# Two chunks' attention outputs times their weights by Strassen's product instead of a plain one, in a kernel of two attention branches

## The chip, the cores and the metric

The kernel runs on one NeuronCore of one Trainium2 chip. The metric is the device time of one execution in microseconds (us), lower is better. The engines are TensorE (PE in the profile; PEld is its weight loading), VectorE (DVE), ScalarE (ACT), GpSimd (POOL) and SyncE (SP), whose queue issues the DMAs.

## The reference

There are two branches over 2048 tokens of width 1024 and 32 heads of 32; their outputs are put side by side. Branch A is the Infini-attention of four segments, not touched here but for its last product `o @ wo`. Branch B is linear attention with a learned feature map:

```python
qkv = (x @ wqkv).reshape(B, S, 3, H, Dh).transpose(2, 0, 3, 1, 4)
q, k, v = qkv[0], qkv[1], qkv[2]
pq = einsum("bhsd,hdf->bhsf", q, w_phi);  pk = einsum("bhsd,hdf->bhsf", k, w_phi)
phi_q = concatenate([softmax(pq), softmax(-pq)], -1)
phi_k = concatenate([softmax(pk), softmax(-pk)], -1)
kv = einsum("bhsf,bhsd->bhfd", phi_k, v);  z = einsum("bhsf->bhf", phi_k)
num = einsum("bhqf,bhfd->bhqd", phi_q, kv)
den = einsum("bhqf,bhf->bhq", phi_q, z)[..., None] + 1e-6
b = (num / den).transpose(0, 2, 1, 3).reshape(B, S, D) @ wo        # the product that changes
return concatenate([a, b], -1)
```

Everything is float32. The kernel splits each float32 operand into two float16 halves, a rounded high one and the rest, and multiplies high by high, high by low and low by high: three products for one.

## The kernel before

**Order.** The work is not written in program order. Every instruction is handed to a planner (`Graph`) with an engine, an assumed duration, a priority `prio` (lower goes first) and the buffers that it reads and writes. `G.run()` simulates the engines with these durations and writes out each engine's instructions in the order that it finds. On the chip every engine then runs its list strictly in that order. The planner also gives out the eight PSUM banks: each request has a kind (`proj`, `misc`, `s`, `pv`, `kv`), `MOST` limits how many of a kind may be held (3, 2, 3, 1, 4) and `KEEP` holds one back for each of the first four. Buffers with the same tag are used in turn; the last number of `G.buf` says how many there are.

**Stages.** First comes branch A's attention, whose output is left in DRAM (`oa_d`). Then come branch B's keys and values (the K stage): 8 pairs `p` of 128-token chunks, each with two Strassen products (keys, then values, for p = 0 to 5; keys alone for 6 and 7), the two-sided softmax of the keys (`expo`), and the sums over tokens of features times values (L1264). Then its queries (the Q stage): 16 chunks `c`. Last is branch A's output product in 8 pairs of chunks, by Strassen's product (L1499).

**Strassen's product here** (Winograd's form): two chunks of 128 rows give a left matrix of 2 x 2 blocks of 128 x 512 (A11, A12, A21, A22), the weights give 2 x 2 blocks of 512 x 512. Seven products of 12 matmuls take the place of eight. They need the forms A11, A12, A22, S1 = A21 + A22, S2 = S1 - A11, S3 = A11 - A21, S4 = A12 - S2, and, of the weights, B11, B21, B22, T1 to T4. Results are gathered in three banks X, Y, Z; intermediate sums are copied out (`keep`) and joined with a later bank (`store`). The query, key and value products (`strassen`, matmuls on L549) and branch A's output have this form already.

**The Q stage.** For an even c the query product of chunks c and c + 1 is made in three `proj` banks. Its priority is P - 1.2 with P = Q0 + c. For each of the four blocks (chunk, half of the heads `hb`) `expo` makes the exponentials `e` (5 buffers) on VectorE and ScalarE. Then per chunk and half: GpSimd multiplies `e` with the key sums (L1414), VectorE reduces (L1417), GpSimd finishes the denominators and scales `e` (L1426), ScalarE and VectorE split it into halves `eh` (tag `kls`, L1432 and L1434), two DMA transposes bring it into `pt` (3 buffers, L1437), and TensorE multiplies it with the key-value sums into a bank `pn` of kind `pv` (L1445). ScalarE and VectorE take `pn` as halves into `ot` (4 buffers, one per chunk, L1449 and L1451). When both halves of the heads are there, `project` multiplies the chunk's 128 x 1024 output with both column halves of `wo` (`product`, matmuls on L359): 2 x 8 x 3 = 48 matmuls of 512 columns. ScalarE copies each bank to `os` (L1329), and SyncE stores it. The priority of `project` is P + 1.1.

**Weights.** `keep_bo(n)` runs in the K stage at p = 1 and 2, once for each column half of branch B's `wo`. It loads 2 MB in two loads to find the scale (absolute sums on ScalarE, L1201), loads them again, makes 8 pairs of halves (`halves`: ScalarE on L386, VectorE on L388, into `kls`) and stores them to `bo_d` (L1210). Before the Q stage they are loaded into slots S4 to S7. Branch A's forms are made in the Q stage (`sizes_out` at c = 1 to 4, `weights` at c = 5, 7, 9, 11; `forms` on L458, L465 and L466): B11, B21 and T1 directly in slots S10, S13 and S14, the other four through `wo_d` in DRAM, loaded at c = 14 (L1402).

## Time and profile before

| | us |
|---|---|
| median of 3 runs | 1761.08 |
| lowest and highest run | 1757.87, 1761.38 |
| the profiled execution, its own time | 1762.63 |
| the profiled execution, its span in the trace | 1760.8 |
| busy in that span: TensorE, VectorE | 1692.6, 1404.1 |
| busy in that span: ScalarE, GpSimd | 1129.7, 968.4 |

In the rows a group of instructions reads: line, engine, operation, written and read tiles, shapes, how many | busy us in total, mean ns of one | idle time of that engine just before them, and what ended it. A row of engines by stage reads: stretch, its length, then the busy us and instructions of each engine, the clock that TensorE was granted (1.00 is full), the share of time that the DMA engines were busy, and GB/s. A row of the timeline reads: start, length, engine, line, operation, how many [idle time before, and its cause]. In a row of waits stand the total us, how many there were and the longest. Matmuls of 512 columns are listed with some 380 ns each, but they overlap: the busy time of a group, divided by its number, is what one costs.

### The profile page before, as it was taken

What the parts mean: (1) busy time and instruction counts of PE and PEld (TensorE: products, weight loads), DVE (VectorE), ACT (ScalarE), POOL (GpSimd) and SP (SyncE); (2) the same over time, 40 slices, a digit from 0 to 9 for tenths busy, and PEclk for the clock granted to TensorE, in tenths of its full rate; (3) what the DMA queues carried; (4) which work ended last, traced back from release to release, by engine and by line L of the source; (5) the groups of instructions that cost most, each with busy time, mean ns of one, the idle gap of its engine ahead of it and who ended that gap; (6) DMA issues with size and microseconds to landing.
All of it is one profiled execution on the core that took longest, in us unless ns stands there. A gap on an engine that the chain in (4) does not pass through costs nothing.

```text
span 1760.8 us, 38488 instructions
## 1 busy us (share of the span) xinstructions
PE 1692.6 (96%) x14456; PEld 1013.5 (58%) x14456; DVE 1404.1 (80%) x3207; ACT 1129.7 (64%) x2063; POOL 968.4 (55%) x1301
## 2 busy tenths in 40 slices
PE   8999999999999999999989999999899999989999
PEld 5767666667776766766744444444444444444444
DVE  5989989899777888788875998996988777677541
ACT  6887886978776787777774656554665544444431
POOL 6445454555757577866773535553578989650000
PEclk8999999999999999999999999999999999999999
DMA  5546546475445444567456343346646666665311
GB/s 191 183 147 178 143 144 182 150 219 170 145 137 152 119 134 122 152 197 184 129 183 254 114 140 137 138 146 236 225 138 168 156 164 147 141 187 159 120 66 66
DMA packets 240842, 275.67 MB, mean 157 GB/s; under 512 B 137488, under 2 KB 190480, under 8 KB 231952
## 3 DMA queue, kind: packets, MB, share of 16 engines
q1 hardware_dynamic: 240656, 273.22, 51.0%
q8 instruction: 113, 1.85, 0.4%
q14 instruction: 73, 0.60, 0.1%
HBM read 145.44 MB, written 85.00 MB: 131 GB/s over the span
## 4 chain that ended last, share of the span: by engine, by line
PE 58%; DVE 19%; ACT 5%; POOL 3%; issue 2%; DMA 1%; SPq 0%; ACTq 0%; DVEq 0%
PE proj L359 19%; PE proj L549 9%; PE proj L1499 5%; PE misc L359 5%; PE s L865 3%; PE pv L901 3%; PE s L767 2%; PE s L1499 2%; DVE s L773 2%; PE s L549 2%; DVE mx L1110 2%; DVE S L388 2%; DVE r L1120 1%; POOL e L1414 1%; PE misc L1499 1%
## 5 line engine op out<-in xcount | busy, mean ns | idle before, releaser
L359 PE MATMUL proj<-S,S 128*128 128x128 f16 (+1 forms) x3072 | 504.0, 300 | 5.2 <-ACT S L386 3.3
L359 PEld LDWEIGHTS <-S 128*128 128x128 f16 x4608 | 331.8, 99 | 154.8 <-issue 10.7
L549 PE MATMUL proj<-S,S 128*128 128x512 f16 x1488 | 351.0, 384 | 17.9 <-ACT cs L555 5.7
L549 PEld LDWEIGHTS <-S 128*128 128x128 f16 x1968 | 189.0, 99 | 237.9 <-issue 19.6
L878 POOL TENSOR_SCALAR_AFFINE_SELECT ph<-ph 128x256 f16<-128x256 f16 (+1 forms) x448 | 196.2, 459 | 178.8 <-DVE ph L872 142.7
L872 DVE SCALAR_TENSOR_TENSOR ph<-s,ph 128x512 f16<-128x512 f32 x320 | 210.5, 682 | 62.1 <-ACT ph L871 60.1
L773 DVE CUSTOM_DVE_ANT_0 s<-s,causal 128x512 f32<-128x512 f32 (+3 forms) x512 | 242.1, 509 | 12.2 <-PE s L767 8.7
L869 ACT ACTIVATE s<-s,bd 128x512 f32<-128x512 f32 x320 | 212.7, 712 | 24.5 <-PE s L865 24.1
L871 ACT ACTIVATE ph<-s 128x512 f16<-128x512 f32 x320 | 190.8, 657 | 1.2 <-PE pv L901 0.5
L359 PE MATMUL misc<-S,ot 128*128 128x512 f16 x768 | 171.7, 381 | 1.5 <-ACT ot L1449 0.9
L1117 ACT ACTIVATE e<-e,sk 128x256 f32<-128x256 f32 x256 | 114.8, 498 | 77.9 <-DVE e L1114 76.7
L359 PEld LDWEIGHTS <-ot 128*128 128x128 f16 x768 | 73.8, 98 | 91.5 <-DVE ot L1451 2.0
L767 PE MATMUL s<-S 96*128 96x512 f16 (+3 forms) x512 | 113.3, 300 | 6.0 <-DVE mt L773 4.2
L865 PE MATMUL s<-S 104*128 104x512 f16 (+3 forms) x512 | 114.4, 302 | 1.9 <-ACT S L795 0.8
L1414 POOL TENSOR_TENSOR e<-e,zb 128x512 f32<-128x512 f32 x64 | 81.6, 1284 | 50.3 <-DVE r L1120 49.7
L359 PE MATMUL proj<-wv,S 128*128 128x128 f16 x1536 | 104.3, 221 | 0.3 <-DVE mt L773 0.3
L901 PEld LDWEIGHTS <-ph 128*128 128x128 f16 x2560 | 87.8, 96 | 19.0 <-POOL ph L878 2.4
L901 PE MATMUL pv<-vl,ph 128*128 128x66 f16 (+1 forms) x2560 | 93.0, 185 | 2.5 <-POOL ph L878 1.6
L1120 DVE TENSOR_REDUCE r<-e 128x32 f32<-128x1024 f32 x64 | 76.8, 1204 | 10.1 <-ACT e L1117 9.8
L549 PE MATMUL s<-S,S 128*128 128x512 f16 x324 | 76.3, 379 | 0.0
L719 ACT ACTIVATE h<-proj,bd 128x512 f16<-128x512 f32 x64 | 47.6, 748 | 44.0 <-PE proj L359 43.8
L773 DVE DVE_READ_ACCUMULATOR2_ANT mt<- 128x1 f32 x512 | 71.9, 140 | 0.0
(313 smaller groups left out, 3268.9 us busy)
## 6 DMA issues: line engine op xcount, KB each, us to landing
S<-h SPq DMA_DIRECT2D x192, 128.0 KB
S<-wf_d SPq DMA_DIRECT2D x21, 1024.0 KB
st<-bwqk SPq DMA_DIRECT2D x64, 256.0 KB
wf_d<-fo SPq DMA_DIRECT2D x48, 256.0 KB
out<-os SPq DMA_DIRECT2D x40, 256.0 KB
wf_d<-oT SPq DMA_DIRECT2D x36, 256.0 KB
S<-xf_d SPq DMA_DIRECT2D x9, 1024.0 KB
S<-aw SPq DMA_DIRECT2D x16, 512.0 KB
```

The source lines that it names most:

```text
L359: op(PE, dur, lambda c=c, a=a, b=b, lv=lv, rv=rv: nc.tensor.matmul(pv(), lv(), rv(), start=(c == 0 and a + b == 0), stop=(c == n - 1 and a ...
L549: op(PE, 0.215, lambda n=n, a=a, b=b, lv=lv, rv=rv: nc.tensor.matmul(ps(), lv(), rv(), start=(start and n == 0 and a + b == 0), stop=(n == ...
L767: nc.tensor.matmul(ps()[:, o:o + 128 * i + 128], st()[0:96, 0, h, 128 * i:128 * i + 128], st()[0:96, 1, h, 0:128 * i + 128], start=True, s ...
L773: dve(0.12 + 0.00113 * n, lambda h=h, i=i, o=o, n=n: nc.vector.tensor_tensor_reduce(ps()[:, o:o + n], ps()[:, o:o + n], causal[:, 512 - n: ...
L865: nc.tensor.matmul(ps()[:, o:o + n], st()[0:104, 1, h, 128 * j:128 * j + 128], st()[0:104, 0, h, 128 * j:512], start=True, stop=True)
L869: act(0.59, lambda: nc.scalar.activation(ps(), ps(), AF.Exp, bias=0.0, scale=bd()[:, 4, i2, 0:1]), r=[(bd, i2)], w=[ps])
L871: act(0.5, lambda: nc.scalar.activation(ph()[:, 0], ps(), AF.Copy, scale=2.0 ** 14), r=[ps], w=[(ph, 0)])
L872: dve(0.6, lambda: nc.vector.scalar_tensor_tensor(ph()[:, 1], ps(), 2.0 ** 14, ph()[:, 0], op0=OP.mult, op1=OP.subtract), r=[ps, (ph, 0)], ...
L878: nc.gpsimd.affine_select(pd, pd, pattern=[[0, n], [1, 128]], compare_op=OP.is_ge, fill=0.0, base=0, channel_multiplier=-1)
L901: nc.tensor.matmul(ps()[:, i, n0:n1], ph()[:, a, o:o + 128], vl()[:, j, h, n0:n1], start=(i == 0 and a == 0), stop=(j == min(i, 2)), skip_ ...
L1117: op(ACT, 0.41, lambda i=i: nc.scalar.activation(e()[:, 4 * i:4 * i + 4], e()[:, 4 * i:4 * i + 4], AF.Exp, bias=0.0, scale=sk()[:, i:i + 1 ...
L1499: op(PE, 0.215, lambda n=n, a=a, b=b: nc.tensor.matmul(ps(), v(a)[:, n, :], wform[w]()[:, b, n, :], start=(start and n == 0 and a + b == 0 ...
```

## The change

- Branch B's output product takes two chunks at a time, in Strassen's form, with the same `project` as branch A's (the body of A's loop moves into it): 7 x 12 = 84 matmuls for two chunks in place of 96, in banks `misc`, `misc` and `s`. Its `keep` copies go to `os` and `kva`. It runs after an odd chunk.
- The forms are made where `pn` lies, now a bank of kind `kv`. Even chunk: each of the two banks is copied to plain float32 (A11 in `kva`, A12 in `ez`) and taken as halves. Odd chunk: the first bank is copied (A21, in a `pt` buffer), turned into S3 by a sum in place and taken; the second is taken as A22 and then turned by three sums in place into S1, S2 and S4, each taken in turn. `take` is the same pair of instructions as before (ScalarE, VectorE); a pair now has seven of them and uses all four `ot` buffers.
- Branch B's weights need seven forms. `sizes_bo` (at p = 0) finds one scale for the whole of `wo`; `weights_bo(j)` (at p = 1 to 4) loads 1 MB, makes seven pairs of halves with four sums on GpSimd, and stores each form's part to `bo_d`. Seven loads of 1 MB into slots KS follow where four were.
- All seven of branch A's weights' forms go through `wo_d`, and all seven are loaded at c = 14, into the slots VS that held the queries' weights.

The core of the diff:

```diff
-    def keep_bo(n, prio):
-        ... (2 x 4 absolute sums; 2 x 4 halves; 2 stores of 1 MB)
+    def sizes_bo(prio):
+        tw = G.buf("b", [128, 16], F32, "ast", 1)
+        for q in range(4):
+            raw = G.buf("b", [128, 4, 512], F32, "zb")
+            ... (load of 1 MB, four absolute sums in place)
+        scale((tw, tw), 16, (wscs, (1, 0), lambda: wsc[:, 1, 0]), prio, "pv", 13)
+    def weights_bo(j, prio):
+        raw = G.buf("b", [128, 4, 512], F32, "zb")
+        for k in range(2):
+            op(SP, 0.6, ... nc.sync.dma_start(raw()[:, 2 * k:2 * k + 2]..., bwo[:, j + 4 * k, :]), ...)
+        def dst(f):
+            ... (kept: one of four places of a "kls" buffer; then a store to bo_d[f, :, :, j, :])
+        forms(WPLAN, lambda k: (raw, k, lambda: raw()[:, k]), dst, (wscs, (1, 0), ...), prio)
...
-        if p in (1, 2):
-            keep_bo(p - 1, P + 0.5)
+        if p == 0:
+            sizes_bo(P + 0.5)
+        if 1 <= p < 5:
+            weights_bo(p - 1, P + 0.5)
...
+    def project(form, wform, kinds, tags, rows, col, sc, prio):
+        ... (mult, keep, store: as in branch A's loop before)
+        X, Y, Z = (bank(k, [128, 512]) for k in kinds)
+        mult(X, "A11", "B11", True)
+        mult(Y, "A12", "B21", True)
+        p1 = keep(X, tags[0])
+        store(p1, rows[0], 0, Y)
+        mult(X, "S2", "T2", False)
+        u2 = keep(X, tags[1])
+        mult(Z, "S1", "T1", True)
+        p5 = keep(Z, tags[2])
+        mult(X, "S3", "T3", False)
+        store(p5, rows[1], 512, X)
+        mult(Z, "S4", "B22", False)
+        store(u2, rows[0], 512, Z)
+        mult(X, "A22", "T4", False)
+        store(keep(X, tags[3]), rows[1], 0)
...
+            for i, f in enumerate(FORMS):
+                wform[f] = G.buf("slot", [128, 2, 4, 512], F16, f"S{VS[i]}")
...
+        def take(ps, f):
+            ... (the next half of an "ot" buffer)
+            op(ACT, 0.48, lambda: nc.scalar.activation(v(0), ps(), AF.Copy, scale=2.0 ** -15), ...)
+            op(DVE, 0.6, lambda: nc.vector.scalar_tensor_tensor(v(1), ps(), 2.0 ** -15, v(0), op0=OP.mult, op1=OP.subtract), ...)
+        def sums(ps, a, b, o):
+            op(DVE, 0.6, lambda: nc.vector.tensor_tensor(ps(), a(), b(), op=o), ...)
+        def plain(ps, tag):
+            t = G.buf("b", [128, 4, 128], F32, *tag)
+            op(ACT, 0.48, lambda: nc.scalar.activation(t(), ps(), AF.Copy), ...)
...
-            pn = bank("pv", [128, 4, 128])
+            pn = bank("kv", [128, 4, 128])
...
+            if c % 2 == 0:
+                if hb == 0:
+                    A11 = plain(pn, ("kva",))
+                    take(pn, "A11")
+                else:
+                    A12 = plain(pn, ("ez",))
+                    take(pn, "A12")
+            elif hb == 0:
+                A21 = plain(pn, ("pt", 3))
+                sums(pn, A11, pn, OP.subtract)
+                take(pn, "S3")
+            else:
+                take(pn, "A22")
+                sums(pn, A21, pn, OP.add)
+                take(pn, "S1")
+                sums(pn, pn, A11, OP.subtract)
+                take(pn, "S2")
+                sums(pn, A12, pn, OP.subtract)
+                take(pn, "S4")
-        project(lambda a, g: (ot, None, ...), bo, c * 128, 1024, P + 1.1)
+        if c % 2:
+            project(form, bof, ("misc", "misc", "s"), (("stage", "os", 1), ("b", "kva", 1), ("stage", "os", 1), ("stage", "os", 1)),
+                    (c - 1, c), 1024, (wo2b, lambda: wo2), P + 1.1)
```

More of the change, by code (lines that the diff above doesn't have):

```diff
@@ new lines, in sizes_bo @@
+        scale((tw, tw), 16, (wscs, (1, 0), lambda: wsc[:, 1, 0]), prio, "pv", 13)
+    def weights_bo(j, prio):
+        raw = G.buf("b", [128, 4, 512], F32, "zb")
+        for k in range(2):
+            op(SP, 0.6, lambda k=k: nc.sync.dma_start(raw()[:, 2 * k:2 * k + 2].rearrange("p a b -> p (a b)"), bwo[:, j + 4 * k, :]),
+               w=[(raw, 2 * k), (raw, 2 * k + 1)], prio=prio, lat=1.0, kb=512)
+        made = []
+        def dst(f):
+            if len(made) % 4 == 0:
+                kept = G.buf("b", [128, 4, 2, 512], F16, "kls")
+            else:
+                kept = made[-1]
+            i = len(made) % 4
+            made.append(kept)
+            return *((kept, (i, a), lambda a=a: kept()[:, i, a]) for a in range(2)), lambda: op(
+                SP, 0.6, lambda: nc.sync.dma_start(bo_d[f, :, :, j, :], kept()[:, i]), r=[(kept, (i, a)) for a in range(2)],
+                w=[(bob, (f, j))], prio=prio, lat=1.5, kb=256)
+        forms(WPLAN, lambda k: (raw, k, lambda: raw()[:, k]), dst, (wscs, (1, 0), lambda: wsc[:, 1, 0]), prio)
@@ L1321, in zv @@
     def zv():
         return zb().rearrange("p a (two s d) -> p (a two) s d", two=2, s=2)
-    def project(o, w, row, col, prio):
-        for n in range(2):
-            ps = bank("misc", [128, 512])
-            product((ps, ps), o, at(w[n]), NG, prio, dur=0.215)
-            os = G.buf("stage", [128, 512], F32, "os", 1)
-            op(ACT, 0.6, lambda os=os, ps=ps, n=n: nc.scalar.activation(os(), ps(), AF.Copy, scale=wo2[:, n:n + 1]),
-               r=[ps, wo2b], w=[os], prio=prio)
-            op(SP, 0.6, lambda os=os, n=n: nc.sync.dma_start(
-                out[row:row + 128, col + 512 * n:col + 512 * n + 512], os()), r=[os], prio=prio, lat=1.5)
@@ L1334, in tile_kernel @@
[L1334 to L1339 removed]
+    FORMS = ("B11", "B21", "T2", "T1", "T3", "B22", "T4")
```

139 lines of the change are left out of this document (60 added, 79 removed).

## The prediction, made before any run of the changed kernel

> **What bounds the kernel now.** I read the page's first part, then the busy time of each engine by stage, then groups of instructions, then the chain of work. The stages, by which lines run when: attention up to about 960 us; the keys' features (K stage) to about 1262, its last pairs overlapped by the first query products; the queries with the projection (Q stage) to 1611; the other branch's output product to the end.
>
> ```profile
> PE 1692.6 (96%) x14456; PEld 1013.5 (58%) x14456; DVE 1404.1 (80%) x3207; ACT 1129.7 (64%) x2063; POOL 968.4 (55%) x1301
> ...
> core 0: us, PE busy (x) PEld busy (x) DVE busy (x) ACT busy (x) POOL busy (x), PEclk, DMA share, GB/s
> 960.00:1180.00 220.00, 205.70 (x1356) 100.77 (x1355) 204.08 (x333) 130.15 (x264) 105.94 (x96) 0.99 0.36 128
> 1222.00:1611.00 389.00, 369.81 (x2494) 178.45 (x2492) 315.60 (x481) 201.97 (x377) 267.86 (x296) 0.99 0.62 170
> ...
> 1050.00:1095.00 45.00, 41.24 (x256) 19.74 (x255) 39.84 (x68) 26.55 (x59) 22.01 (x20) 0.96 0.46 158
> 1095.00:1138.00 43.00, 39.36 (x272) 19.25 (x269) 42.85 (x70) 25.11 (x48) 20.41 (x21) 1.00 0.40 141
> 1180.00:1222.00 42.00, 40.63 (x281) 20.19 (x280) 28.11 (x47) 17.58 (x34) 13.88 (x13) 1.00 0.68 257
> 1300.00:1480.00 180.00, 175.56 (x1186) 83.12 (x1185) 142.20 (x203) 94.56 (x167) 155.93 (x164) 1.00 0.63 155
> 1480.00:1570.00 90.00, 88.95 (x593) 42.21 (x591) 67.64 (x105) 40.11 (x72) 52.60 (x66) 1.00 0.58 153
> 1570.00:1611.00 41.00, 35.04 (x232) 16.66 (x231) 29.83 (x41) 17.68 (x27) 14.16 (x18) 0.92 0.66 193
> 1611.00:1760.80 149.80, 145.77 (x676) 65.88 (x674) 58.97 (x86) 49.59 (x75) 0.00 (x0) 1.00 0.23 83
> ...
> 1222.00:1557.00 335.00, 321.76 (x2182) 155.67 (x2181) 273.75 (x421) 176.02 (x334) 247.07 (x270) 1.00 0.62 168
> 1557.00:1597.00 40.00, 34.04 (x255) 16.42 (x250) 30.87 (x45) 19.94 (x34) 20.79 (x26) 0.91 0.52 153
> ```
>
> Over the whole span TensorE leads with 96%, but the stages differ. In the Q stage TensorE is the bound: 175.56 of 180 us and 88.95 of 90, with VectorE at 79% and 75%. In the K stage two engines share the bound: VectorE 204.08 of 220 (92.8%), TensorE 205.70 (93.5%). The chain of waits says the same:
>
> ```profile
> by line: PE misc L359 39.6%; PE proj L549 25.3%; PE pv L1445 5.4%; issue 3.1%; DVE kls L1434 2.5%; ACT e L1117 2.0%; DMA out<-os 2.0%; DMA pt<-kls 1.8%; DVE mx L1110 1.7%; DVE e L1112 1.6%; ACT os L1329 1.5%; DVE ot L1451 1.5%; POOL e L1414
> ...
> by line: PE proj L549 24.5%; PE s L549 10.7%; DVE S L388 8.2%; DVE mx L1110 5.3%; DVE kls L388 5.2%; DVE r L1120 4.1%; PE misc L549 4.1%; issue 4.0%; DVE pt L1257 3.9%; DVE e L1114 3.7%; PE kv L1264 3.6%; DVE ot L1150 3.0%; DVE e L1112 2.8%
> ```
>
> The first is 1425 to 1600, where TensorE's projection (L359) and query products (L549) hold 65%; the second is 960 to 1180, where VectorE's lines are woven into TensorE's.
>
> **The change, part by part.** The rows that carry the terms:
>
> ```profile
> L359 PE MATMUL misc<-S,ot 128*128 128x512 f16 x768 | 171.7, 381 | 1.5 <-ACT ot L1449 0.9 <-DVE ot L1451 0.5
> L1451 DVE SCALAR_TENSOR_TENSOR ot<-pv,ot 128x512 f16<-128x512 f32 x32 | 21.7, 678 | 4.9 <-ACT ot L1449 4.7
> L559 DVE TENSOR_TENSOR proj<-cs,proj 128x512 f32<-128x512 f32 x12 | 8.3, 688 | 6.8 <-PE proj L549 5.0 <-ACT ot L1449 1.2 <-ACT cs L555 0.6
> L1512 DVE SCALAR_TENSOR_TENSOR st<-misc,wsc,st 128x512 f32<-128x512 f32 x8 | 6.0, 751 | 26.1 <-PE misc L1499 26.1
> L1449 ACT ACTIVATE ot<-pv 128x512 f16<-128x512 f32 x32 | 18.7, 587 | 22.3 <-PE pv L1445 22.3
> L1329 ACT ACTIVATE os<-misc,wo 128x512 f32<-128x512 f32 x32 | 21.8, 681 | 28.2 <-PE misc L359 21.9 <-issue 3.9 <-DMA out<-os 2.2
> L388 DVE SCALAR_TENSOR_TENSOR kls<-zb,wsc,kls 128x512 f16<-128x512 f32 x16 | 12.0, 805 | 0.0
> L388 DVE SCALAR_TENSOR_TENSOR S<-st,pst,S 128x512 f16<-128x512 f32 x5 | 7.8, 1568 | 0.0
> L458 POOL TENSOR_TENSOR h<-st,h 128x512 f32<-128x512 f32 x5 | 8.7, 1731 | 10.9 <-DVE S L388 10.9
> L458 POOL TENSOR_TENSOR h<-h,h 128x512 f32<-128x512 f32 x4 | 5.1, 1268 | 9.4 <-issue 8.3 <-POOL r L1123 0.6 <-POOL ot L1137 0.5
> ```
>
> TensorE, Q stage. The projection had 768 products in 171.7 us, 0.2236 each. Now 8 pairs x 7 forms x 12 = 672: 96 fewer, **-21.5 us** of TensorE.
>
> VectorE, Q stage. The low halves go from 32 to 56: 24 x 0.678 = 16.3. Four sums a pair in PSUM: 32 x 0.688 (L559, the same kind of sum) = 22.0. Three joins with a kept product a pair: 24 x 0.751 (L1512) = 18.0. Together **+56.3 us**.
>
> ScalarE, Q stage. 24 more high halves and 24 plain copies, 48 x 0.587 = 28.2; the 32 evacuations stay 32. 202 + 28 of 389 is 59%, off the path unless it is late for VectorE: L1451's one large wait, 4.7 of its 4.9 us, is on ScalarE.
>
> What becomes of the -21.5 and the +56.3. I split the stage at 1557, where the last query product ends. Up to there fall the forms of seven pairs in eight (38.3 x 7/8 = 33.5) and the joins of six (18.0 x 6/8 = 13.5): VectorE's 273.75 us become 320.8, TensorE's 321.76 lose 6/8 of 21.5 and become 305.6. The bound changes engine. If VectorE fills as in the K stage (92.8%), the 335 us become 320.8 / 0.928 = 346, +11. If it fills as TensorE does here when it binds (175.56 / 180 = 97.5%), 329, -6. The first end is the nearer by kind, VectorE among the same partners; the second by place. I take 95%: 337.7, **+3**. GpSimd, 155.93 of 180 us, gets nothing new here but waits for VectorE, so a denser VectorE delays it too; that speaks against more than 95%.
>
> The end of the Q stage. Forms S1 to S4 hang on the pair's last product. S1 follows after a copy, a low half, a sum, a copy and a low half: 0.587 + 0.678 + 0.688 + 0.587 + 0.678 = 3.2 us; S2 and S4 each 1.95 later.
>
> ```profile
> 1556.41 0.86 PE L1445 MATMUL pv<-pt,st 128*64 128x128 f16 x24
> ...
> 1584.35 0.32 PE L1445 MATMUL pv<-pt,st 128*64 128x128 f16 x2 [3.85 <-DMA pt<-kls]
> 1585.73 1.38 PE L1445 MATMUL pv<-pt,st 128*64 128x128 f16 x22 [1.06 <-DMA pt<-kls]
> 1587.05 4.50 PE L359 MATMUL misc<-S,ot 128*128 128x512 f16 x14
> ...
> 1595.65 0.86 PE L1445 MATMUL pv<-pt,st 128*64 128x128 f16 x24
> 1596.44 15.28 PE L359 MATMUL misc<-S,ot 128*128 128x512 f16 x70
> 1611.56 2.75 PE L1499 MATMUL proj<-S,ot 128*128 128x512 f16 x12
> ...
> 1064.82 4.49 PE L549 MATMUL proj<-S,S 128*128 128x512 f16 x14 [3.64 <-ACT S L386]
> ...
> 1106.09 3.19 PE L549 MATMUL proj<-S,S 128*128 128x512 f16 x14
> ```
>
> Behind the last product stood 15.28 us of projection. Now 3.2 us of waiting (A11 and A12 can run before) and five forms, 60 x 0.22 = 13.2 (0.22 from 14 in 3.19 and 12 in 2.75 us), together 16.4: **+1**. Before it, from 1557 to 1597, the last pair's chain sets the time and VectorE has 9 of 40 us to spare for the 9 of new work: no cost taken, and none of the 5 us that TensorE is spared there counted. S4 at 7.1 us is covered by S1, S2 and S3. The final product's first forms use the same `ot` buffers, the first free once A11 and A12 are multiplied, so its start stays close behind.
>
> Handing over between pairs. The plain copy of A11 shares its buffer `kva` with u2, so the next pair's first bank is not released until u2's store has left. Behind that copy on ScalarE stand the next chunk's exponentials. The loop is about 3 x 1.95 us of forms, four dozen products (10.6) and a store of a few us, near 25 us out of some 42 a pair (335 / 8): no cost taken, and rival D if this cover is gone. Less lead, too: projecting a first chunk alone no longer fills TensorE while the second is being made; its cover is the next pair's query products, 84 x 0.22 = 18 us.
>
> K stage. The weights' halves go from 16 to 28 on VectorE and ScalarE: 12 x 0.75 (12.0 / 16) = +9 us of VectorE; GpSimd gets 16 sums of 1.27 to 1.73. The 16 size passes stay, earlier. Three of the four new batches fall before 1180, 21 halves for 16, +3.8 us; the fourth can go where VectorE has 14 us free (28.11 of 42). VectorE suffers beside GpSimd's sums: L388 from `st` takes 1.568 against 0.75 from `zb`. If half of 12 sums cost 0.8, +5. The upper end is 8.8 / 0.928 = +9.5. The lower end is a gain: before, the halves came in bursts, and the 3.64 us wait of TensorE for L386 at 1061 and its slow products after (4.49 us for 14, against 3.19) may vanish, -5. I take **+3**, in the upper half, since VectorE has no room there (42.85 of 43).
>
> Transfers.
>
> ```profile
> L1210 SPq DMA_DIRECT2D bo_d<-kls x4: 326/326/327, 1031.3 to 1118.5; - x4
> ...
> PE pv L1445 <- DMA pt<-kls: 7.1, 5, 3.8
> ...
> 1539.17 3.81 SPq L1402 DMA_DIRECT2D S<-wo_d  x2
> ...
> 1552.43 0.53 SPq L1402 DMA_DIRECT2D S<-wo_d  x1
> ```
>
> In K, 12 issues become 40: 28 x 0.33 = 9 us of SyncE over 200, hidden. In Q come 3 MB more of the first weights' forms, 12 more stores and 3 MB more of the second's, 9 MB: 53 us at the stage's 170 GB/s, on engines that are 62% busy. They are issued on the queue of the transposes, which cost TensorE 7.1 us. Bounds 0 and another 7; I take **0**, as the seven late loads have from 1552 to 1611 where four stood. That last product, 672 products after 1611, is unchanged.
>
> Sum: +3 +1 +3 +0 = **+7 us**. The profiled execution took 1762.63 us with a span of 1760.8; the median of the runs is 1761.08, the same within 0.1%. Forecast 1768.
>
> **The rivals.**
>
> B, faster: VectorE packs its new work and TensorE's saving comes through. At 97.5% the stretch to 1557 loses 6 us, at the 99.6% of the stretch from 1095 (42.85 of 43) 320.8 / 0.996 = 322, so 13; TensorE's own floor, 305.6 / 0.975 = 313.4, would be -21.6. With +1 at the end and the K stage's sums in the free 14 us, the times are 1756, 1749 and 1740; I give 1752. It decides at a fill of 320.8 / 335 = 95.8%. For it: VectorE has been that full. Against it: in that stretch TensorE stood at 92%, and everything here depends on three engines at once.
>
> C, no change: the loads cancel, VectorE at 95 to 96% and the K stage hidden: 1759 to 1764.
>
> D, much slower: TensorE waits for S1 in most pairs, since the next pair's query products find their three banks still unread. A wait of 4 us, and slow products behind it: 14 took 4.49 and 4.50 us after waits of 3.64 and 3.85 (4.9 with the second), against 3.19, so 1.3 us more. Eight times 5.3 is 42: -21.5 + 42 + 3 gives 1785, six of eight 1774. For it: the granted clock fell to 0.96 and 0.92 in the stretches with those two waits. Against it: with a lead of a whole product few waits reach 3.6 us.
>
> The Trainium skill, "TensorE: Matmul & The Clock Gate", Part 1 (The HAM clock gate), says that an idle window of about 3.4 us halves TensorE's clock until it has been busy that long again. By its figures 3.4 us at half rate would lose an estimated 1.7 us for each such wait rather than 1.3, and D would be some 1788. The two waits agree with the rule in kind.
>
> **How the numbers follow.** A (VectorE binds) 0.42, 1768, its own range 1762 to 1778; B 0.30, 1742 to 1757; C 0.14; D 0.14, 1774 to 1786. About 0.2% (3.5 us) can be told from no change here. A gives slower 0.37 and same 0.05; B faster 0.30; C same 0.13 and faster 0.01; D slower. Faster 0.31, same 0.18, slower 0.51. The range, 1748 to 1784, leaves out the lower part of B and the top of D.
>
> **What would show it.** Right: VectorE at 93% or more up to the last query product, ahead of TensorE, which drops to about 91%; TensorE's waits there end on VectorE's or ScalarE's `ot`; 672 projection products; L388 on `kls` 28 times in the K stage, which ends some 3 us later. Wrong: TensorE still at 97% with a stage 10 us or more shorter (B), or a granted clock under 0.95 over several stretches (D). The prediction fails if VectorE's sums in PSUM are much off 0.69 us, or if the order lets VectorE fill beyond 96%.

## The result, and the profile after

The changed kernel takes 1783.29 us (median of 4 runs, 1782.39 to 1785.39) against 1759.8 for the kernel before beside it: slower by 23.5 us, ratio 1.0135, interval 1.0123 to 1.0148. The forecast was 1768. The direction was right, and the time lies inside the range, at its upper edge; the increase is more than three times the one forecast.

The page of the changed kernel, first part:

```profile
PE 1683.5 (95%) x14358; PEld 1008.5 (57%) x14358; DVE 1461.4 (82%) x3296; ACT 1161.0 (65%) x2123; POOL 994.6 (56%) x1317
```

The attention stage, whose code is the same, ended at 946.7 us in the profiled execution before and at 941.9 in the one after, so I compare stage lengths and not positions. I cut at four events: the last attention product, the last sum over keys (`kv<-ot`), the last query product (L549), and the last product of a block with the key sums (`pn`). The last six of the 32 `pn` come after the last query product; I call that third part the chain. First the kernel before, then the changed one:

```profile
946.70:1272.00 325.30, 303.42 (x2059) 150.99 (x2057) 288.29 (x473) 182.87 (x378) 150.09 (x136) 0.99 0.47 171
1272.00:1556.50 284.50, 277.47 (x1802) 131.17 (x1802) 223.97 (x336) 142.19 (x258) 219.33 (x245) 1.00 0.62 156
1556.50:1596.50 40.00, 34.04 (x267) 16.67 (x268) 31.37 (x45) 19.44 (x33) 20.79 (x26) 0.91 0.53 152
1596.50:1760.80 164.30, 160.27 (x744) 72.48 (x742) 69.94 (x103) 56.10 (x86) 0.00 (x0) 1.00 0.28 98
```

```profile
941.90:1278.20 336.30, 307.45 (x2044) 153.59 (x2043) 300.25 (x480) 185.13 (x378) 177.50 (x152) 0.97 0.49 177
1278.20:1564.60 286.40, 270.74 (x1740) 126.65 (x1738) 258.80 (x398) 165.82 (x309) 218.39 (x245) 0.98 0.68 178
1564.60:1613.90 49.30, 30.74 (x253) 15.52 (x250) 36.36 (x55) 20.61 (x36) 20.23 (x26) 0.83 0.72 179
1613.90:1780.70 166.80, 160.04 (x736) 71.74 (x732) 77.16 (x115) 59.66 (x92) 0.00 (x0) 0.99 0.26 92
```

K stage +11.0, queries +1.9, chain +9.3, end +2.5: together +24.7 us after the attention, close to the 23.5 of the medians.

The same rows say what became of TensorE's saving. Multiply each stage's TensorE time by its granted clock (the column after GpSimd's) and add up: 769 us of work at full clock before, some 747 after. That is about 21.6 less, and the prediction had 21.5 (an estimate: the clock is a mean over the whole stage, pauses included, and printed to 0.01, worth some 3 us in the long stages). So the saving is there. Against it stand two things: the time lost to a clock below 1.00, 6 us before and 21.5 after, and the time in which TensorE had nothing to do, 38.9 us before and 69.8 after. -21.6 + 15.4 + 30.9 = +24.7.

The end of the query stage shows both. Start, length, product, and what TensorE waited for:

```profile
1564.47 5.34 PE L1346 MATMUL misc<-S,ot 128*128 128x512 f16 x24
1569.75 0.86 PE L1515 MATMUL kv<-pt,st 128*64 128x128 f16 x24
1576.63 1.49 PE L1515 MATMUL kv<-pt,st 128*64 128x128 f16 x24 [6.03 <-DMA pt<-kls]
1588.96 1.03 PE L1346 MATMUL s<-S,ot 128*128 128x512 f16 x2 [10.83 <-ACT ot L1465]
...
1613.12 0.86 PE L1515 MATMUL kv<-pt,st 128*64 128x128 f16 x24 [1.70 <-DMA pt<-kls]
1613.92 2.76 PE L1346 MATMUL misc<-S,ot 128*128 128x512 f16 x12
1619.42 4.45 PE L1346 MATMUL s<-S,ot 128*128 128x512 f16 x12 [2.74 <-ACT ot L1465]
```

After the 6.03 us the products are slow: the 24 of a `pn` take 1.49 us and not 0.86. After 2.74 us twelve take 4.45 and not 2.75. Before the change, 22 and then 74 projection products ran between the first three `pn` of this part, a chunk's 48 as soon as its own two blocks were taken; now a pair has 24 (A11, A12) until S1 is there, and the other five forms come behind S1. In bank X, S3 and A22 stand behind S2. Behind S1 TensorE hardly stops: from 1588.96 to the end of the chain are 25.0 us, with one listed pause of 1.70. So the chain grew in front of S1, where TensorE stood still for 6.03 and 10.83 us.

### The profile page after: what moved, and what is told of

The parts are those of the page before. It is cut to its first block, busy times and chain, and to the rows that moved or that the text cites. A ratio compares the mean times of both kernels' runs of the same rounds, so it can differ in the third digit from the quotient of the medians.

```text
span 1780.7 us, 38628 instructions
## 1 busy us (share of the span) xinstructions
PE 1683.5 (95%) x14358; PEld 1008.5 (57%) x14358; DVE 1461.4 (82%) x3296; ACT 1161.0 (65%) x2123; POOL 994.6 (56%) x1317
## 4 chain that ended last, share of the span: by engine, by line
PE 55%; DVE 22%; ACT 3%; issue 3%; POOL 3%; DMA 1%; SPq 0%; DVEq 0%; ACTq 0%; POOLq 0%
PE proj L359 19%; PE proj L549 7%; PE misc L1346 6%; PE proj L1346 5%; PE s L1346 4%; PE s L865 3%; PE pv L901 3%; DVE mx L1110 2%; PE s L767 2%; DVE r L1120 2%; DVE S L388 2%; DVE s L773 2%; DVE kls L388 1%; DVE e L1114 1%; DVE e L1112 1%
## 5 line engine op out<-in xcount | busy, mean ns | idle before, releaser
L549 PE MATMUL proj<-S,S 128*128 128x512 f16 x1488 | 354.4, 384 | 19.4 <-ACT cs L555 9.0
L549 PEld LDWEIGHTS <-S 128*128 128x128 f16 x1968 | 189.3, 99 | 243.8 <-issue 24.1
L869 ACT ACTIVATE s<-s,bd 128x512 f32<-128x512 f32 x320 | 212.7, 711 | 23.8 <-PE s L865 23.5
L1346 PEld LDWEIGHTS <-ot 128*128 128x128 f16 x1056 | 102.5, 99 | 152.5 <-ACT ot L1465 22.8
L1346 PE MATMUL misc<-S,ot 128*128 128x512 f16 x576 | 136.1, 382 | 4.1 <-DVE os L1358 2.7
L1346 PE MATMUL s<-S,ot 128*128 128x512 f16 x288 | 74.9, 396 | 19.9 <-ACT ot L1465 19.7
L549 PE MATMUL s<-S,S 128*128 128x512 f16 x324 | 77.5, 385 | 0.9 <-ACT cs L555 0.9
```

Source lines behind the costliest of these rows:

```text
L549: op(PE, 0.215, lambda n=n, a=a, b=b, lv=lv, rv=rv: nc.tensor.matmul(ps(), lv(), rv(), start=(start and n == 0 and a + b == 0), stop=(n == ...
L869: act(0.59, lambda: nc.scalar.activation(ps(), ps(), AF.Exp, bias=0.0, scale=bd()[:, 4, i2, 0:1]), r=[(bd, i2)], w=[ps])
L1346: op(PE, 0.215, lambda n=n, a=a, b=b: nc.tensor.matmul(ps(), v(a)[:, n, :], wform[w]()[:, b, n, :], start=(start and n == 0 and a + b == 0 ...
```

## The experiments

Four questions: do the parts add up, what makes the K stage longer, what makes the chain longer, and how much is only the order that the planner wrote. My first theory was the prediction's A: VectorE, with 56 us of new work, sets the query stage. Rivals: the costs lie in the weights' forms (K stage, transfers), or in waits.

### The parts alone

`e1_k_alone` is the kernel before with the new forms of `wo` and the plain projection, on four of those forms:

```diff
-        if p in (1, 2):
-            keep_bo(p - 1, P + 0.5)
+        if p == 0: sizes_bo(P + 0.5)
+        if 1 <= p < 5: weights_bo(p - 1, P + 0.5)
```

> The kernel before with the new weights' work in the K stage alone: one scale, four batches of seven forms with GpSimd's sums, stored to DRAM; the projection stays the plain product with four of these blocks, so branch B's output is of other weights. Theory K (the K stage's share lasts to the end): the last key sum comes 5.8 us later in the changed kernel, so +4 to +7 over the kernel before, about 1765. Rival H (it is hidden, since TensorE binds afterwards and has a queue of projections to work on): within 1.5 us of the kernel before.

Measured: 1774.78 us, ratio 1.0085 (1.0070 to 1.0100), +15.9. Theory K, with two to four times its size. Its stages, K, queries, chain:

```profile
944.10:1282.20 338.10, 310.47 (x2057) 154.96 (x2055) 301.65 (x482) 187.84 (x386) 175.35 (x152) 0.97 0.48 172
1282.20:1567.70 285.50, 279.33 (x1802) 131.98 (x1800) 233.29 (x335) 143.94 (x262) 222.46 (x245) 0.99 0.63 160
1567.70:1609.80 42.10, 34.29 (x266) 16.52 (x264) 33.02 (x46) 19.31 (x33) 20.73 (x26) 0.88 0.54 134
```

K +12.8, and VectorE +13.4 in it.

`e2_a_dram_alone` is the kernel before with all seven of branch A's forms through DRAM, loaded late:

```diff
-            for i, f in enumerate(SECOND):
+            for i, f in enumerate(FORMS):      # all seven, loads of 1 MB at c = 14
```

> The kernel before with only this part: all seven of branch A's weights' forms through DRAM, 12 stores and 3 loads of 1 MB more, into the slots of the queries' weights. Forecast's theory: hidden, within 2 us of the kernel before. Rival L (late loads delay the transposes of the last chunks, behind which the changed kernel's TensorE waited 6.03 us): +3 to +9.

Measured: 1766.64 us, ratio 1.0042 (1.0025 to 1.0059), +7.7. That is the time of rival L. The K stage is as before (325.3); the queries have 1.8 more, the chain 5.5 (seven blocks fall into it here and six before, so the two are best read together, +7.3):

```profile
1267.10:1553.40 286.30, 277.72 (x1778) 131.07 (x1778) 223.00 (x334) 141.85 (x257) 214.53 (x245) 0.99 0.62 167
1553.40:1598.90 45.50, 34.21 (x289) 16.63 (x288) 33.16 (x48) 19.29 (x34) 20.38 (x26) 0.89 0.80 204
```

The DMA engines are busy 0.80 of the chain, against 0.53 before. But rival L's mechanism does not show here: in this chain TensorE waits 0.53 us for a transpose and 10.6 us for takes. The first of these stood on ScalarE behind a copy that waited for GpSimd (first line; the take follows at 1570.66):

```profile
1569.70 1.06 ACT L1433 ACTIVATE kls<-e 128x1024 f16<-128x1024 f32 x1 [4.99 <-POOL e L1427]
...
1571.29 0.65 PE L359 MATMUL misc<-S,ot 128*128 128x512 f16 x2 [4.17 <-ACT ot L1450]
1578.40 5.80 PE L359 MATMUL misc<-S,ot 128*128 128x512 f16 x18 [6.45 <-DVE ot L1452]
```

The planner wrote another order for this version too, and it was not timed in a second one; how the 7.7 us come about stays open. In the changed kernel the issues show where loads and blocks meet:

```profile
1559.01 7.38 SPq L1507 DMA_TRANSPOSE pt<-kls  x3
1566.48 1.02 SPq L1449 DMA_DIRECT2D S<-wo_d  x2
1567.60 0.39 SPq L1550 DMA_DIRECT2D e<-oa_d  x1
1568.04 3.28 SPq L1507 DMA_TRANSPOSE pt<-kls  x1
```

The transpose for which TensorE then waits 6.03 us (until 1576.63) is issued right behind two loads of 1 MB, and its issue takes 3.28 us where half of all take 1.26 or less. Before, the last such load went out at 1552.43, 23 us ahead of the next transposes. How much of the 6.03 us is due to the loads, no run separates.

15.9 + 7.7 = 23.6, the whole increase. If the two parts simply add up in the changed kernel, the Strassen projection itself, which saves the 21.5 us of TensorE, adds and gains about nothing on top. No run has it alone.

### The query stage: is it VectorE?

`e3_no_sums` is the changed kernel without the four sums of a pair:

```diff
-                sums(pn, A11, pn, OP.subtract)
-                sums(pn, A21, pn, OP.add)
-                sums(pn, pn, A11, OP.subtract)
-                sums(pn, A12, pn, OP.subtract)
```

> The changed kernel without the four sums in PSUM of each pair (the forms S1 to S4 are taken from unsummed banks, so branch B's output is not the reference's). VectorE loses 32 instructions of 0.69 us, 22 us. Theory V (VectorE's load binds the Q stage, as forecast): most of it comes back, 12 to 20 us, 1764 to 1771. Theory T (the loss sits at the end of the stage, in instructions that wait in the engines' fixed order, and VectorE's load is not the bound): only the chains at the end shorten, 3 to 8 us, 1775 to 1780.

Measured: 1779.54 us, ratio 1.0109 (1.0092 to 1.0126), 3.7 less than the changed kernel. VectorE loses 15 us in the queries and the stage 1.3:

```profile
1280.20:1565.30 285.10, 271.10 (x1715) 125.19 (x1714) 243.43 (x373) 162.69 (x304) 218.76 (x245) 0.98 0.71 179
1565.30:1615.20 49.90, 36.21 (x288) 16.85 (x286) 35.33 (x55) 25.07 (x43) 19.59 (x27) 0.86 0.73 181
```

Seven blocks and not six fall into its chain, so queries and chain together are the fairer reading: 335.0 us against 335.7. The time is theory T's. Theory A falls: VectorE's load is not what holds the query stage. (The order is another one here as well; `s_a_115` below says the same, with 10 us more in the stage at no more VectorE work.) No engine is full there: TensorE 95%, VectorE 90%, GpSimd 76% in the changed kernel.

### The K stage

`e4_no_pool_sums` leaves out GpSimd's 16 sums for the forms of `wo`:

```diff
-        forms(WPLAN, ...
+        forms([(None, k, f) for _, k, f in WPLAN], ...
```

> The changed kernel without GpSimd's 16 sums in the making of branch B's weights' forms (the forms are plain blocks, so the output is not the reference's). VectorE's 28 halves there took 1.14 us on average against 0.75 us of the 16 halves in the kernel before. Theory P (GpSimd's sums slow VectorE's halves beside them): the halves fall to 0.75 to 0.85 us, 8 to 10 us of VectorE, and the kernel gets 3 to 6 us faster, about 1779. Rival: they stay above 1.0 us and the time stays within 1.5 us, since something else (the other instructions on GpSimd, or the halves' own reads) slows them.

Measured: 1782.09 us, ratio 1.0122 (1.0107 to 1.0137); K stage 335.0, 1.3 shorter, the halves still 1.10 us each: the rival. Then what slows them? The group in the changed kernel, and two slow ones as VectorE and GpSimd show them:

```profile
L388 DVE SCALAR_TENSOR_TENSOR kls<-zb,wsc,kls 128x512 f16<-128x512 f32 x28 | 30.8, 1137 | 0.0
```

```profile
1020.32 0.74 DVE L388 SCALAR_TENSOR_TENSOR kls<-zb,wsc,kls 128x512 f16<-128x512 f32 x1
...
1021.64 4.07 DVE L388 SCALAR_TENSOR_TENSOR kls<-zb,wsc,kls 128x512 f16<-128x512 f32 x2
```

```profile
1021.14 1.70 POOL L458 TENSOR_TENSOR zb<-zb 128x512 f32<-128x512 f32 x1 [0.60 <-DVE kls L388]
1022.80 2.36 POOL L1236 TENSOR_TENSOR e<-e,r 128x1024 f32<-128x1024 f32 x1
```

One half takes 0.74 us by itself; two take 4.07 where GpSimd ends a sum (L458) and multiplies features (L1236, in both kernels) at the same time. Before the change 15 of the 16 halves took 0.74 us and one, beside a sum on GpSimd, 1.76 (805 ns on average); spread over four batches, ten of the 28 took 0.88 to 2.50, each beside GpSimd. GpSimd's own operations grow too (L458 1.26 to 1.70, L1236 1.91 to 2.36). The Trainium skill, "SBUF — State Buffer", Who interferes with whom, states that a VectorE operation with two SBUF inputs and a GpSimd operation that reads SBUF exclude each other for a whole instruction; the half reads two tiles, and the rows agree.

`e9_bo_pool` takes the low halves off VectorE:

```diff
-        forms(WPLAN, ..., dst, (wscs, (1, 0), ...), prio)
+        ... (ScalarE scales raw in place, two passes)
+        forms(WPLAN, ..., dst, None, prio, POOL)
```

> The changed kernel with the low halves of wo's forms in the K stage taken off VectorE: ScalarE scales each raw block (16 passes more), GpSimd subtracts (28 of some 1.3 us). Theory K (the K stage grew because VectorE, nearly full, has 12 halves more and waits for GpSimd in each that falls beside a GpSimd operation): VectorE loses 30.8 us in the K stage and the stage falls by 8 to 15, to 321-328; time 1768 to 1776. Rival M (the K stage grew for another reason: four more batches of loads and weights' forms in the order, whoever computes them, or TensorE's waits for ScalarE): stage 333-340, time 1780 to 1786.

Measured: 1782.07 us, ratio 1.0129 (1.0114 to 1.0144). Between the two: K stage 332.3, 4.0 shorter, given back in the queries (+2.2) and the chain (+2.5). VectorE's busy time falls by 12 us and not by 30.8, for others now collide with GpSimd: the low halves of the features (`pt<-e,pt`, L1272 here) take 1.13 us instead of 0.82.

`e10_bo_late` puts the batches at p = 3 to 6:

```diff
-        if 1 <= p < 5: weights_bo(p - 1, P + 0.5)
+        if 3 <= p < 7: weights_bo(p - 3, P + 0.5)
```

> The changed kernel with the batches of wo's forms two steps later (steps 3 to 6 of the key projection instead of 1 to 4), where VectorE is less full (28 of 42 us busy in the stretch after 1180 before the change). Theory K: the K stage loses 4 to 8 us, to 328-332; time 1776 to 1780. Rival M: stage 334-338, time 1781 to 1786.

Measured: 1784.1 us, ratio 1.0149 (1.0122 to 1.0175). A miss for both: K stage 338.8, longer. The queries fall to 276.6 and the chain grows to 57.0: the query products end 10 us sooner and the blocks do not, so that eight of them and not six fall into the chain.

`e11_16_halves` and `e17_16_no_sums` go back to 16 halves, the second without GpSimd's sums as well:

```diff
-        forms(WPLAN, ...)
+        ... (halves for four of the seven forms; the other three stored from the same buffers)
```

> The changed kernel with the halves of only four of the seven forms of wo in each of the four batches of the K stage (16 low and 16 high halves, as many as before the change); the other three forms are stored from those four, so all loads, stores, sums and size passes remain. It leaves out 12 low halves of VectorE and 12 high ones of ScalarE. Theory K (the number of halves on VectorE makes the K stage longer): K stage back to 326-329, TensorE's waits there down by some 5 us and its clock back to 0.99; time 1773 to 1777. Rival D (four batches instead of two, with their loads, stores and sums, wherever the halves are): K stage 333-337, time 1780 to 1784.

> The changed kernel with 16 low and 16 high halves of wo's forms in the key stage, as before the change, and without GpSimd's 16 sums for them (it leaves both out; loads, stores and size passes stay). Only the key stage is read, since the query stage's order changes with it. Theory K+ (halves and sums collide on VectorE and GpSimd, together they are the 11 us): key stage 325 to 328. Rival R (half of the 11 us belongs to the four batches, their loads and stores and where they fall): 329 to 332.

Measured: K stage 331.6 (between theory K and rival D) and 329.5; times 1796.41 us (1.0222, 1.0207 to 1.0237) and 1773.36 (1.0099, 1.0073 to 1.0124). K, queries and chain of the second, with eight blocks in the chain:

```profile
943.90:1273.40 329.50, 305.60 (x2055) 152.85 (x2053) 291.86 (x470) 179.17 (x366) 152.27 (x137) 0.98 0.50 180
1273.40:1545.40 272.00, 256.76 (x1650) 119.69 (x1647) 250.16 (x388) 160.98 (x300) 210.47 (x242) 0.99 0.72 184
1545.40:1605.00 59.60, 43.76 (x347) 20.68 (x345) 46.02 (x65) 26.72 (x45) 27.49 (x30) 0.89 0.68 167
```

So of the +11.0, the twelve halves with their collisions hold 4.7, halves and sums together 6.8 (other orders of the same instructions move this stage by about 1 us). The 4.2 that remain belong to the four batches otherwise; their halves still fall badly (16 of 1.23 us). Which of loads, stores, size passes and places it is, was not separated: rival R in size. The time of e11, 13 us above the changed kernel with less work, is a matter for the section on orders.

### The chain

`e5_p5_in_cs` relieves the single buffer `os`:

```diff
-            project(form, bof, ..., (("stage", "os", 1), ("b", "kva", 1), ("stage", "os", 1), ("stage", "os", 1)),
+            project(form, bof, ..., (("stage", "os", 1), ("b", "kva", 1), ("b", "cs", 4), ("stage", "os", 1)),
```

> The changed kernel with one of the three kept products of a pair (P5) in the four buffers `cs` instead of the single buffer `os`, so that ScalarE's next copy to `os` does not wait for the store of the one before (8.15 us from its issue; 9.9 us of ScalarE's waits between 1227 and 1626). Theory B (that wait, behind which stand the last blocks' halves in ScalarE's fixed order, makes the chain long): chain of the last six blocks 41 to 45 instead of 49.3, time 1774 to 1779. Rival F (the chain is long by the fixed order itself, the take behind the copies that wait for GpSimd): chain 48 to 51, time 1781 to 1786.

Measured: 1963.82 us, ratio 1.1164 (1.1147 to 1.1180). A miss for both. The queries take 468.8 us (chain 49.9), with TensorE waiting for transposes nearly once a block:

```profile
PE kv L1515 <- DMA pt<-kls: 93.3, 29, 10.3
```

The buffers `cs` pass between the query products and the forms of A's weights; that a product which waits for its store does not fit among them is my reading, not shown. With such a stage before it, the chain says nothing on `os`.

`e12_measured` gives the planner the durations of the trace; `e13_a22_first` forces ScalarE's copies of block 14 behind the take of A22; `e16_s1_first` also VectorE's sums of block 15 behind S1:

```diff
-            op(DVE, 1.13, lambda eh=eh, ...      # low halves
+            op(DVE, 1.46, lambda eh=eh, ...      # e12, and 15 more such figures
```

```diff
-               r=[e], w=[(eh, (hb, 0))], prio=P)
+               r=[e, *(last22 if c == 14 else [])], w=[(eh, (hb, 0))], prio=P)          # e13, e16
-               r=[(e, ("x", a))], w=[(dn, a)], prio=P)
+               r=[(e, ("x", a)), *(first if c == 15 else [])], w=[(dn, a)], prio=P)     # e16
```

> The changed kernel with the planner's durations in the query stage set to what the trace shows (takes 0.60 and 0.69 instead of 0.48 and 0.60, low halves 1.46 instead of 1.13, GpSimd's products 1.4 and 2.06, issue of a transpose 1.26 instead of 0.60 with 3.0 until it is there): the same instructions in another order. Theory F (the order written from short durations puts takes behind copies that are late on the chip, and TensorE waits there): pauses of TensorE over 1.4 us between the first query product and the last of the six blocks fall from nine (35 us together) to five or fewer, the chain to 42-45, time 1773 to 1778. Rival S (the waits come from the chain product, sum, take, take itself, whatever the order): chain 48 to 52, time 1781 to 1787.

> The changed kernel with one order forced: ScalarE's copies for block 14's halves come behind the take of A22 of the pair before, which stood behind them when TensorE waited 10.83 us. Theory F: that wait falls to 4 us or less, chain of the last six blocks 42 to 45, time 1775 to 1779. Rival S (block 14's and 15's own halves come later by as much, and their transposes are waited for instead): chain 48 to 52, time 1781 to 1786, with a wait on the transposes in place of the other.

> The changed kernel with two orders forced at the end of the query stage: block 14's high halves behind A22's high half (as in e13), and block 15's sums of the feature maps behind S1's high half, so that VectorE takes A22, adds S1 and takes it before it waits for GpSimd. Theory G (five of the seven products of a pair stand behind S1, and S1's takes stand in VectorE's and ScalarE's fixed orders behind work that waits for GpSimd): the wait for S1 falls from 9.3-10.8 to 5 us or less, chain 42 to 47, time 1777 to 1781. Rival H (GpSimd's own work for blocks 14 and 15 sets the end, and it now comes later): the wait falls, the waits for the transposes of block 15 grow by as much, chain 48 to 52, time 1781 to 1786.

Measured: e12 1800.17 us (1.0240, 1.0225 to 1.0256), chain 50.4, queries 299.0. e13 1784.44 (1.0162, 1.0142 to 1.0181), chain 51.5. e16 1784.81 (1.0161, 1.0142 to 1.0180), chain 50.1. Theory F falls. The first fence, ScalarE in the changed kernel, shows why A22 was late (its product had ended at 1578.12); the second and third, ScalarE and VectorE in e13, where the wait went (product ended at 1579.64):

```profile
1579.88 1.06 ACT L1502 ACTIVATE kls<-e 128x1024 f16<-128x1024 f32 x1 [5.15 <-POOL e L1496]
1584.61 1.06 ACT L1502 ACTIVATE kls<-e 128x1024 f16<-128x1024 f32 x1 [3.67 <-POOL e L1496]
1585.57 0.58 ACT L1465 ACTIVATE ot<-kv 128x512 f16<-128x512 f32 x1
```

```profile
1579.68 0.60 ACT L1465 ACTIVATE ot<-kv 128x512 f16<-128x512 f32 x1 [3.56 <-PE kv L1515]
```

```profile
1582.70 0.69 DVE L1487 TENSOR_REDUCE dn<-e 128x16 f32<-128x512 f32 x1 [2.61 <-POOL e L1484]
...
1586.46 0.63 DVE L1466 SCALAR_TENSOR_TENSOR ot<-kv,ot 128x512 f16<-128x512 f32 x1
```

In e13 ScalarE takes A22 at once, 7.4 us sooner after the product, and VectorE's low half of it still comes 6.8 us after the product, behind sums that wait for GpSimd. TensorE's wait for S1 falls from 10.83 to 9.28 (e13) and 7.85 us (e16), and the chain does not get shorter. That is rival S in e13 (the last wait for a transpose grows from 1.70 to 3.27 us); theory G is not borne out by e16, whose wait stayed above 5 us because VectorE's low half of A22 stood behind a reciprocal that waited 3.99 us for GpSimd. Rival H's numbers came out there, its mechanism did not: block 15's transposes, waited for 1.70 us in the changed kernel, are not waited for at all. Nor does GpSimd's last scaling mark the end: it comes 27.6 us after the last query product in the changed kernel, and 30.8 before the change, when the chain was 40.0. In e16 GpSimd waited 4.81 us for the sums put off and ended 6 us later, and the chain grew by 0.8. What took the gain in e16 is the stretch behind S1: S1 comes 3.0 us sooner after the last query product, and from there to the chain's end are 28.8 us instead of 25.0, with TensorE busy for 27.6 of them (23.3): twelve more products are listed ahead of the last `pn`, at a clock of 0.90 instead of 0.93. Which order would bring S1 early and keep the rest, is not settled.

### The order

`e7_scatter` moves one planner figure by 0.01, which leaves the orders almost as they were:

```diff
-            op(DVE, 1.13, lambda eh=eh, ...
+            op(DVE, 1.14, lambda eh=eh, ...
```

> The changed kernel with one figure of the planner moved by 0.01 (the low halves of the last blocks planned at 1.14 us and not 1.13): no instruction is added or dropped, only the order may differ. Theory W (the new costs sit in the work, not in this one order): within 3 us of the changed kernel's 1783, K stage 336 +-2, last six blocks' chain 49 +-3. Rival O (the 9 us of the chain, or the 11 of the K stage, are this order's bad luck): the chain or the K stage comes out 5 us or more apart from those, and the time with it.

Measured: 1787.05 us, ratio 1.0152 (1.0134 to 1.0170), a little above theory W's 3 us, with the same stages (336.3, 286.3, 49.4). A weak test, so both kernels were re-ordered by a figure that counts in every block (`s_a_115` the changed one, `s_b_115` the one before), and the kernel before by measured durations (`b_measured`, as e12):

```diff
-        op(DVE, 1.13, lambda: nc.vector.tensor_reduce(r(), e(), axis=AX.X, op=OP.add), ...
+        op(DVE, 1.15, lambda: nc.vector.tensor_reduce(r(), e(), axis=AX.X, op=OP.add), ...
```

> The changed kernel, one planner figure of the feature maps (the sum over the exponentials, 1.13 in the plan, 1.20 in the trace) set to 1.15: the same instructions, the key and query stages in another order. Theory W (the costs are the work's): 1779 to 1788. Rival O (a large part of the 23.5 us is the luck of the orders): outside that by more than 4 us, on either side.

> The kernel before with the same figure at 1.15. Theory W: 1755 to 1764. Rival O: slower than that by 5 us or more, since the order of the kernel before was a lucky one; the two re-ordered kernels then stand less than 18 us apart.

> The kernel before the change with the same measured durations given to its planner in the query stage: the same instructions in another order. Theory F: its few pauses (3.85 and 1.06 us on transposes in the last blocks) shrink, time 1754 to 1758, a version faster than both kernels. Rival: order makes no difference where 24 to 48 products of a block always stand ready, 1758 to 1763.

Measured: s_a_115 1798.83 us (1.0234, 1.0213 to 1.0255); s_b_115 1756.93 (0.9987, 0.9975 to 0.9999); b_measured 1765.74 (1.0040, 1.0025 to 1.0054), slower and not faster, a miss for both, with stages of 325.2, 284.8 and 44.0 (seven blocks in its chain). K, queries and chain of `s_a_115`, then of `s_b_115`:

```profile
943.60:1279.30 335.70, 307.63 (x2044) 153.19 (x2043) 301.19 (x480) 186.53 (x378) 177.98 (x152) 0.97 0.49 177
1279.30:1575.70 296.40, 272.47 (x1740) 126.99 (x1738) 256.06 (x396) 166.76 (x310) 216.83 (x245) 0.97 0.66 174
1575.70:1627.10 51.40, 34.68 (x265) 16.42 (x262) 38.98 (x58) 21.62 (x37) 20.30 (x26) 0.80 0.66 166
```

```profile
941.50:1265.70 324.20, 306.42 (x2059) 152.88 (x2058) 290.65 (x473) 182.12 (x378) 150.16 (x136) 0.98 0.48 171
1265.70:1548.40 282.70, 276.27 (x1799) 131.06 (x1798) 226.58 (x335) 141.78 (x258) 224.16 (x245) 1.00 0.60 159
1548.40:1587.80 39.40, 34.55 (x267) 16.67 (x266) 32.73 (x47) 19.10 (x33) 20.67 (x26) 0.91 0.53 136
```

The K stage keeps its distance in other orders (335.7 against 324.2, and 336.3 in e12 against 325.2): that cost is the work's. The chain's distance is 9.3 in the first orders, 12.0 here and 6.4 between e12 and b_measured: it stays, but its size is in part the order's. The queries are what the order moves most: 286, 296 and 299 us for the same instructions of the changed kernel (in `s_a_115` TensorE waits 4.38 us for a transpose and 5.34 for a load of the queries, `S<-xf_d`); 283 to 285 in all orders of the kernel before. `s_a_115` lies outside theory W's range, as rival O has it, but the two kernels move apart and not together: 23.5 us in the first orders, 42 here, 34 between e12 and b_measured. So luck of the order does not explain the increase; the order that was timed is a good one for the changed kernel. It would fit e11 too, whose K stage fell and whose queries took 299.8; that was not tested in a second order.

Last, the four `ot` buffers, which hold one pair's forms and held four chunks. `e14_b_depth2` makes the kernel before wait as the changed one must; `e15_ot5` gives the changed one a fifth:

```diff
         ot = G.buf("b", [128, 2112], F16, "ot", 4)
+        ring.append(ot)                                  # e14
+        if len(ring) > 2:
+            ot.prev = (ring[-3], *ot.prev[1:])
```

```diff
-        e = G.buf("b", [128, 16, 2, 32], F32, "e", 5)
+        e = G.buf("b", [128, 16, 2, 32], F32, "e", 4)    # e15; r as well, and "ot" 5
```

> The kernel before, in the query stage each block's take made to wait for the projection of the block two before it (the `ot` buffers let it run four ahead): the depth that the changed kernel has, whose pair of blocks fills all four. No instruction is added. Theory B (that depth is what starves TensorE in the last blocks and in the pauses of the query stage): query stage and chain together 330 to 336 instead of 324.5, time 1765 to 1772. Rival N (the planner never runs more than two blocks ahead, or TensorE has other work): 1757 to 1763.

> The changed kernel with five `ot` buffers instead of four, and four instead of five of the feature maps' `e` and `r`, whose room that takes. Theory B: the next pair's first takes no longer wait for the pair before, chain of the last six blocks 42 to 46, query stage 278 to 284, time 1770 to 1778. Rival N: 1780 to 1790, with waits on `e` in the key stage (stage over 338) if four of them are too few.

Measured: e14 1759.45 us, ratio 1.0000 (0.9989 to 1.0012); e15 1794.63 (1.0206, 1.0184 to 1.0227), K 337.3, queries 288.5, chain 55.4. Theory B falls on the first for the kernel before, unless its planner never ran further ahead (rival N leaves that open). The second agrees, though four `e` may cost time of their own.

No version came near 1759.8 with the change in it. Faster than both kernels is only s_b_115, the kernel before in another order, by 0.13% with an interval that ends at 0.01%.

## Why the prediction was right or wrong

The direction was right. The sum was +7: +3 for the queries, +1 for the end, +3 for the K stage, and nothing for the chain and the transfers. The stages came out at +1.9, +2.5, +11.0 and +9.3: the chain, put at nothing, and the K stage, put too low, hold the miss.

- **Query stage, +3 forecast, +1.9 measured.** The sum came out by luck, its reason did not. In the prediction's stretch, up to the last query product, the changed kernel has:

```profile
1227.00:1565.00 338.00, 317.52 (x2115) 153.61 (x2114) 308.26 (x484) 197.17 (x376) 247.71 (x270) 0.97 0.67 188
```

  The 338 us are those forecast. But VectorE's busy time rose to 308.26 and not to 320.8, so that it stood at 91% and not at 95%; TensorE was ahead of it, at 94% and a clock of 0.97. The new halves, sums and joins have the durations that were said, one by one; but a row's mean includes the stretch in which an instruction overlaps the next (two sums of 0.69 us, L1487, take 1.22 in a row), so packed instructions cost less than the sum of their means. That is part of the difference. Without 15 us of VectorE the stage is as long (e3). That VectorE takes over as the bound is not so. What the stage shows instead is that query products and blocks have come apart: in e10 and e17 the query products end 10 to 14 us sooner, two more blocks are left, and the chain is 8 to 10 longer. What holds the blocks there, no run singled out. (A slip without weight: L1451's 4.7 us on ScalarE, called one large wait, are three.)
- **K stage, +3 forecast, +11.0 measured.** The mechanism was right, the term mis-sized. A half was put at 0.75 us (12.0 / 16); the 28 took 1.10 (30.8 / 28). The row that told it was quoted (the same operation from `st`, 1.568 us), and I spread that over only half of twelve. The collisions are with work that was there already as well, so all 28 are exposed: VectorE's halves cost 18.8 us more, not 9. Halves and sums were shown to hold 6.8 of the 11; the other 4.2 stay open.
- **The chain, 0 forecast, +9.3 measured.** This is the step that failed most. "VectorE has 9 of 40 us to spare for the 9 of new work: no cost taken" counts busy time where it matters when a take comes in its engine's in-order queue: A22's low half came 8.7 us after its product, and TensorE stood still for 10.83. The cover that was counted on, the next pair's query products, has ended by then. Of the 9.3, the forms of `wo` alone bring 2.1 (e1) and A's late loads 5.5 (e2, with one block more in its chain).
- **Transfers, 0 forecast (0 to 7), +7.7 measured in e2**, 5.5 of them in the chain. The size is a little above the upper bound. "The seven late loads have from 1552 to 1611" asked when the loads are needed, and not what else they meet. That they delay the transposes, the reason given for the bound, did not show in e2's waits; its mechanism stays open.
- **The end, +1 forecast, +2.5 measured.** The wait for S1 is 2.74 us there (3.2 forecast); the products after it run at a lower clock, 12 in 4.45 us.
- **The rivals.** D, TensorE waiting for S1 with a falling clock, had the right time (1774 to 1786) and half of the mechanism. Idle time and clock hold the whole increase once the saving is counted (+30.9 and +15.4). But pauses of over 1.4 us for S1 stand in four of the eight pairs (3.65, 1.76, 10.83 and 2.74 us, 19 together), not in six to eight; most of the others stand in the K stage (eight, 17 us) and in front of transposes. In all there are 16 such pauses, 51 us together, up to the last blocks' products, where the kernel before has 6 with 15 us. B asked that TensorE's saving come through; it was eaten. C, no change, needed the K stage's cost hidden; it was not.
- **The clock.** The prediction weighed the Trainium skill, "TensorE: Matmul & The Clock Gate", Part 1: an idle window of about 3.4 us halves the clock. In kind the rows agree. But a shorter pause was enough here. Two stretches of 3.41 us of the changed kernel, each with what follows it (the clock stands third from the end):

```profile
1264.55:1267.96 3.41, 0.68 (x5) 0.11 (x2) 3.08 (x6) 3.17 (x9) 2.15 (x2) 1.00 0.35 79
1267.96:1274.78 6.82, 5.84 (x52) 5.50 (x53) 6.68 (x16) 2.49 (x4) 4.01 (x4) 0.50 0.10 40
1616.12:1619.53 3.41, 0.67 (x4) 0.18 (x3) 3.34 (x7) 0.76 (x2) 0.00 (x0) 1.00 0.47 120
1619.53:1622.94 3.41, 3.41 (x9) 1.08 (x9) 3.40 (x6) 1.66 (x3) 0.00 (x0) 0.50 0.70 264
```

  Pauses of 2.26 and 2.74 us, with TensorE busy for some 0.7 of 3.41 us, were followed by half the clock. The prediction's "with a lead of a whole product few waits reach 3.6 us" therefore asked for too long a wait.

## What to carry to other kernels

Cost new work by the rows of the same operation beside the same neighbours, with its slow cases counted in full, and ask of each moved or added transfer what it meets late in its stage, not only when it is needed. Fewer matmuls need not gain where they also take away the products that covered a wait: here five of a pair's seven products wait for the pair's last block, TensorE stood idle for it, and the clock fell. Where a planner writes the order, time both kernels in a second order before a difference in one stage is put down to the change.

## What the runs showed of the hardware

- A VectorE half with two SBUF inputs took 0.74 us alone and up to 2.50 beside a GpSimd sum and a multiplication of 128x1024; GpSimd's multiplication grew from 1.91 to 2.36 us in such a place.
- Work taken off VectorE and given to GpSimd came back in VectorE's other operations: of 30.8 us, 12 were gained (e9).
- TensorE's granted clock was 0.50 for 3.41 and 6.82 us behind pauses of 2.74 and 2.26 us. With eight pauses of 1.55 to 2.96 us in the K stage (five before the change, one of them 3.64), its mean clock there was 0.97 instead of 0.99; with two of 6.03 and 10.83 us in the chain, 0.83 instead of 0.91. Over the whole that cost an estimated 15 us (busy time times clock, by stage).
